# Loading the second MLP weight in five pieces instead of four at the end of a decode block

## The chip, the cores and the metric

One NeuronCore of a Trainium2 chip runs the whole program. The time is the device time of one execution in microseconds (us); "fast" executions are those outside the chip's slower state, and only they are compared. Times from the start of a trace ("at 80.41") count from the first instruction of the profiled execution. A trace spans some 84 us where the device time is some 86. A load is split over 16 DMA engines and counted by 16 increments; it has landed when the last of them has come. Landing times below are taken from these increments in the traces.

## The reference

A decode step of one token for four sequences: adaptive layer norm, cached sliding-window attention, a residual, a second layer norm, and a two-layer MLP with ReLU. Only the last part is touched:

```
def _B_ref(x, w1, w2):            # x [4,1,512], w1 [512,1792], w2 [1792,512]
    h = einsum('bsd,df->bsf', x, w1)
    h = maximum(h, 0)
    return einsum('bsf,fd->bsd', h, w2)
x = x + gb * _B_ref(h, B_w1, B_w2)
```

The inputs are about 32 MB (caches in the window, five weights, all bf16) and each is read once.

## The kernel before

All large loads are issued by SyncE on one queue, in the order in which they are used: k, w_mod, wq, more k, v, wo, w1, and last w2. w2 has 14 blocks of 128 rows. A piece of `e` blocks is laid out so that partition q gets `e` neighbouring rows, one packet of `e` KB. The columns of w1 are then read with step `e`, so that hidden unit and w2 row meet on the same partition.

```
W2_CHUNKS = [(0, 6), (6, 5), (11, 2), (13, 1)]
for (m0, e) in W2_CHUNKS:
    nc.sync.dma_start(out=w2_dst[:, m0 * D:(m0 + e) * D],
                      in_=B_w2[m0 * P:(m0 + e) * P, :].rearrange("(q e) n -> q (e n)", e=e))
...
def w1_cols(t, m):
    m0, e = [ch for ch in W2_CHUNKS if ch[0] <= m][-1]
    return w1_sb[:, t, m0 * P + m - m0:(m0 + e) * P:e]          # step e
...
def ffn1(m0, m1):         # u = w1 columns of blocks m0..m1, then three VectorE operations into uT32
    u_ps = psA.tile(...)
    for m in range(m0, m1):
        for t in range(DT):                                     # 4
            nc.tensor.matmul(out=u_ps[:, m - m0]..., lhsT=w1_cols(t, m), rhs=ab[:, t]..., ...)
    ...
def ffn2(m0, m1):         # z += u block x w2 block, four column groups
    for m in range(m0, m1):
        for nh in range(NH):                                    # 4
            nc.tensor.matmul(out=z_ps[nh * CG:(nh + 1) * CG, :], lhsT=uT32[:, m, :],
                             rhs=w2_sb[:, m, nh * DH2:(nh + 1) * DH2], ...)

for (m0, m1) in [(0, 6), (6, FT)]:
    ffn1(m0, m1)
for (m0, e) in W2_CHUNKS:
    ffn2(m0, m0 + e)
nc.vector.tensor_tensor(out=zg[:], in0=z_ps[:], in1=gb2[:], op=ALU.mult)
nc.vector.tensor_tensor(out=res[:], in0=zg[:], in1=x12_ps[:], op=ALU.add)
nc.sync.dma_start(out=out..., in_=res[::BS, :])
```

Of the kernel before, what the change touches and what calls it, by code (L numbers as in the profile page):

```python
# [17 lines left out]
def kernel(  # L18
# [23 lines left out]
    FT = Dff // P  # L42
# [75 lines left out]
    w2_sb = w12[:, DT * Dff:DT * Dff + FT * D].rearrange("p (m n) -> p m n", m=FT)  # L118
    nc.sync.dma_start(out=w1_sb, in_=B_w1.rearrange("(p t) n -> p t n", t=DT))

    W2_CHUNKS = [(0, 6), (6, 5), (11, 2), (13, 1)]
    assert sum(e for _, e in W2_CHUNKS) == FT
    w2_dst = w12[:, DT * Dff:DT * Dff + FT * D]
    for (m0, e) in W2_CHUNKS:
        nc.sync.dma_start(out=w2_dst[:, m0 * D:(m0 + e) * D],
# [323 lines left out]
    def w1_cols(t, m):  # L449
        m0, e = [ch for ch in W2_CHUNKS if ch[0] <= m][-1]  # L450
        return w1_sb[:, t, m0 * P + m - m0:(m0 + e) * P:e]
# [3 lines left out]
    def ffn1(m0, m1):  # L455
        u_ps = psA.tile([P, m1 - m0, 2, B], f32, tag="t", name=f"u_ps_{m0}")
        for m in range(m0, m1):
            for t in range(DT):
                nc.tensor.matmul(out=u_ps[:, m - m0].rearrange("p s b -> p (s b)"), lhsT=w1_cols(t, m),  # L459
                                 rhs=ab[:, t].rearrange("p s b -> p (s b)"), start=(t == 0), stop=(t == DT - 1))  # L460
        us = work.tile([P, m1 - m0, B], f32, name=f"us_{m0}")
        nc.vector.tensor_tensor(out=us[:], in0=u_ps[:, :, 0, :], in1=rstd2[:].unsqueeze(1).to_broadcast([P, m1 - m0, B]),
                                op=ALU.mult)
        nc.vector.tensor_tensor(out=us[:], in0=us[:], in1=u_ps[:, :, 1, :], op=ALU.add)
        nc.vector.tensor_scalar_max(out=uT32[:, m0:m1, ::BS], in0=us[:], scalar1=0.0)

    def ffn2(m0, m1):
        for m in range(m0, m1):
            for nh in range(NH):
                nc.tensor.matmul(out=z_ps[nh * CG:(nh + 1) * CG, :], lhsT=uT32[:, m, :],  # L470
                                 rhs=w2_sb[:, m, nh * DH2:(nh + 1) * DH2],
                                 start=(m == 0), stop=(m == FT - 1), tile_position=(0, nh * CG))

    for (m0, m1) in [(0, 6), (6, FT)]:
        ffn1(m0, m1)
    for (m0, e) in W2_CHUNKS:
        ffn2(m0, m0 + e)
# [36 lines left out]
```

## Time and profile before

| | before |
|---|---|
| device time, median of 3 (lowest to highest) | 85.94 us (85.81 to 85.98) |
| DMA queue of the loads: packets, MB, share of 16 engines | 4052, 31.99, 91.7% |
| TensorE matmuls busy | 57.5 us, 68% |
| w1 has landed / last piece of w2 has landed | 75.96 / 80.41 us |
| last group of ffn2's matmuls starts | 80.45 us |

The share of TensorE is an average over stages and says little.

### The profile page before, as it was taken

How to read it: one execution, taken by the hardware profiler on the slowest of the kernel's cores; microseconds unless marked ns; L12 is line 12 of the kernel's file. 1: busy time of each engine (PE TensorE's matmuls, PEld its weight loads, DVE VectorE, ACT ScalarE, POOL GpSimd, SP SyncE). 2: the span in 40 equal slices, each digit the busy share in tenths (PEclk: the TensorE clock that was granted, in tenths of full speed). 3: DMA queues.
4: the chain of work that ended last, by engine and by line, in shares of the span. 5: the costliest groups of instructions: out<-in, count | busy, mean ns of one | idle time of the engine just before them, and what ended most of it. 6: DMA issues, size and time to landing. Idle time of an engine off the chain costs nothing.

```text
span 84.1 us, 2367 instructions
## 1 busy us (share of the span) xinstructions
PE 57.5 (68%) x1064; PEld 47.4 (56%) x1064; DVE 26.4 (31%) x73; ACT 23.5 (28%) x37; POOL 5.2 (6%) x20
## 2 busy tenths in 40 slices
PE   0029940499729899999999329996454478598840
PEld 0029940248629739977778029996452058588720
DVE  0144480030330103645665768500003020241420
ACT  2314670003020004977798196300000010001000
POOL 6980000000000000000000000000000000000000
PEclk9999999957955555999999995696555555555555
DMA  0999998999999999999999999999999999999500
GB/s 2 333 401 452 503 421 386 444 421 444 421 394 405 433 433 413 413 413 425 425 413 409 425 425 421 405 433 421 425 409 409 425 432 425 413 398 406 210 0 2
DMA packets 4077, 32.13 MB, mean 382 GB/s; under 512 B 476, under 2 KB 612, under 8 KB 996
## 3 DMA queue, kind: packets, MB, share of 16 engines
q1 hardware_dynamic: 4052, 31.99, 91.7%
q8 instruction: 8, 0.13, 0.6%
q10 hardware_dynamic: 16, 0.01, 0.0%
q14 instruction: 1, 0.01, 0.0%
HBM read 31.99 MB, written 0.00 MB: 381 GB/s over the span
## 4 chain that ended last, share of the span: by engine, by line
DMA 64%; PE 25%; DVE 3%; issue 2%; SPq 1%; ACT 1%; DVEq 0%
DMA w<-in_B_w_dram 24%; DMA v<-in_A_v_cache_dram 24%; DMA wmod_sb<-in_w_mod_dram 16%; PE ktp L202 9%; PE qT_ps L302 4%; PE sc_ps L214 4%; PE mT L253 2%; PE mT L255 2%; PE z_ps L470 2%; PE m_ps L236 2%; SPq L81 1%; PE m_ps L239 1%; PE gb_ps L244 1%; PE st_ps_var L269 1%; ACT lnv L286 0%
## 5 line engine op out<-in xcount | busy, mean ns | idle before, releaser
L202 PEld LDWEIGHTS <-k 128*128 128x128 bf16 x256 | 17.3, 110 | 3.9 <-issue 2.5
L202 PE MATMUL ktp<-ident_k,k 128*128 128x128 bf16 x256 | 18.4, 241 | 1.2 <-DMA k<-in_A_k_cache_dram 1.2
L207 ACT COPY kT<-ktp 128x1024 bf16<-128x1024 bf16 x16 | 15.5, 1016 | 13.2 <-PE ktp L202 12.1
L205 DVE COPY kT<-ktp 128x1024 bf16<-128x1024 bf16 x16 | 11.1, 691 | 11.6 <-PE ktp L202 11.3
L340 PE MATMUL oT_ps<-pT,v 128*128 128x16 bf16 x256 | 7.3, 172 | 2.5 <-issue 1.9
L340 PEld LDWEIGHTS <-v 128*128 128x128 bf16 x256 | 7.1, 100 | 2.7 <-issue 2.0
L214 PE MATMUL sc_ps<-kT,qpad 128*32 128x512 bf16 x64 | 5.6, 445 | 0.4 <-DVE qpad L306 0.4
L357 PE MATMUL pT_ps<-ident_bf,p_rep 128*128 128x128 bf16 x32 | 3.1, 278 | 2.9 <-DVE p_rep L351 2.9
L357 PEld LDWEIGHTS <-p_rep 128*128 128x128 bf16 x32 | 2.7, 127 | 3.4 <-DVE p_rep L351 3.4
L302 PE MATMUL qT_ps<-hT,wq_sb 128*128 128x4 bf16 x128 | 3.6, 166 | 1.4 <-DVE ab L295 1.4
L302 PEld LDWEIGHTS <-wq_sb 128*128 128x128 bf16 x128 | 3.5, 104 | 1.5 <-issue 1.5
L236 PE MATMUL m_ps<-wmod_sb,siluT 128*32 128x512 bf16 x16 | 1.3, 435 | 4.4 <-DMA wmod_sb<-in_w_mod_dram 4.4
L409 ACT COPY y<-y_ps 128x256 f32<-128x256 f32 x1 | 0.4, 372 | 11.4 <-DVE y L408 11.4
L404 PE MATMUL y_ps<-wo_sb,o 128*32 128x512 bf16 x16 | 2.1, 619 | 2.0 <-DMA wo_sb<-in_A_wo_dram 1.1
L177 PE MATMUL tp<-ident_bf,cx_sb 8*128 8x8 bf16 x4 | 0.3, 168 | 4.5 <-DMA cx_sb<-in_A_x_dram 4.5
L236 PEld LDWEIGHTS <-siluT 128*32 128x32 bf16 x16 | 0.4, 95 | 4.7 <-issue 4.5
L382 DVE TENSOR_TENSOR oT_sb<-oT_ps,rb 128x128 bf16<-128x128 f32 x1 | 0.3, 292 | 8.6 <-PE oT_ps L340 8.6
L416 PEld LDWEIGHTS <-wo_sb 128*128 128x128 bf16 x64 | 2.5, 121 | 0.6 <-DMA wo_sb<-in_A_wo_dram 0.6
L416 PE MATMUL y_ps<-o,wo_sb 128*128 128x4 bf16 x64 | 2.4, 173 | 0.5 <-DMA wo_sb<-in_A_wo_dram 0.5
L177 PEld LDWEIGHTS <-cx_sb 8*128 8x128 bf16 x4 | 0.2, 110 | 4.5 <-issue 4.5
L351 DVE TENSOR_TENSOR p_rep<-e_sb,mi 128x512 int32<-128x512 int32 x4 | 2.5, 685 | 0.7 <-ACT e_sb L346 0.7
L459 PE MATMUL u_ps<-ab,w 128*128 128x8 bf16 x56 | 2.4, 181 | 0.4 <-DMA w<-in_B_w_dram 0.4
(107 smaller groups left out, 57.0 us busy)
## 6 DMA issues: line engine op xcount, KB each, us to landing
k<-in_A_k_cache_dram SPq DMA_DIRECT2D x8, 1024.0 KB, 25.8
v<-in_A_v_cache_dram SPq DMA_DIRECT2D x8, 1024.0 KB, 19.9
wq_sb<-in_A_wq_dram SPq DMA_DIRECT2D x2, 2048.0 KB, 18.0
wo_sb<-in_A_wo_dram SPq DMA_DIRECT2D x4, 1024.0 KB, 19.9
wmod_sb<-in_w_mod_dram SPq DMA_DIRECT2D x1, 3072.0 KB, 13.7
w<-in_B_w_dram SPq DMA_DIRECT2D x1, 1792.0 KB, 21.7
w<-in_B_w_dram SPq DMA_DIRECT2D x1, 768.0 KB
w<-in_B_w_dram SPq DMA_DIRECT2D x1, 640.0 KB, 20.1
```

The source lines that it names most:

```text
L202: nc.tensor.transpose(out=tp[:, ii, :], in_=k_tiles[gi][:, iq * IQ + ii, :], identity=ident_k)
L205: nc.vector.tensor_copy(out=dst, in_=tp[:])
L207: nc.scalar.copy(out=dst, in_=tp[:])
L214: nc.tensor.matmul(out=sc_ps[hw * CG:(hw + 1) * CG, half * HALF:(half + 1) * HALF], lhsT=qpad[:, b, par, hw, :], rhs=kT[:, half * (NI // 2 ...
L236: nc.tensor.matmul(out=m4_ps[k * CG:(k + 1) * CG, :], lhsT=siluT32[:, t, :], rhs=wmod_sb[:, t, k * D:(k + 1) * D], start=(t == 0), stop=(t ...
L302: nc.tensor.matmul(out=qT_v[:, hq, :], lhsT=wq_sb[:, t, hq * Dh:(hq + 1) * Dh], rhs=hT[:, t, :], start=(t == 0 and hq == 0), stop=(t == DT ...
L340: nc.tensor.matmul(out=oT_ps[:, hw, par].rearrange("p b r -> p (b r)"), lhsT=v_tiles[h][:, i, :], rhs=pT[:, i, c0:c0 + B * rep], start=(fi ...
L351: nc.vector.tensor_tensor(out=p_w[:, ws, :], in0=e_w[:, ws].unsqueeze(2).to_broadcast([P, WQ // 2, B]), in1=mi4[:].unsqueeze(1).to_broadca ...
L357: nc.tensor.transpose(out=tp[:, ii, :], in_=p_rep[:, i // 2, :, i % 2], identity=ident_bf[:])
L404: nc.tensor.matmul(out=y4_ps[q0:q0 + CG, :], lhsT=o4[:, l, g % 2, g // 2, :], rhs=wo_sb[:, g, l, :], start=(g == 0 and l < 4), stop=(g == ...
L416: nc.tensor.matmul(out=y_ps[:, m, :], lhsT=wo_sb[:, g, l, m::DT], rhs=o4[:, l, g % 2, g // 2, 0:B], start=False, stop=(g == NP - 1 and l = ...
L459: nc.tensor.matmul(out=u_ps[:, m - m0].rearrange("p s b -> p (s b)"), lhsT=w1_cols(t, m), rhs=ab[:, t].rearrange("p s b -> p (s b)"), star ...
```

## The change

The first two pieces, 6 and 5 blocks, become three of 4, 4 and 3, so that ffn2 has fewer blocks to do behind each landing. The last two pieces stay. ffn1's two halves are cut at the border of a piece again, now 8 and 6.

```
-    W2_CHUNKS = [(0, 6), (6, 5), (11, 2), (13, 1)]
+    W2_CHUNKS = [(0, 4), (4, 4), (8, 3), (11, 2), (13, 1)]
...
-    for (m0, m1) in [(0, 6), (6, FT)]:
+    for (m0, m1) in [(0, 8), (8, FT)]:
         ffn1(m0, m1)
```

## The prediction

> **What bounds the kernel now.** I read the page first (shares, slices, the DMA queue), then the chain that ended last in order of time, then the list of DMA issues, then narrow timelines of the last two microseconds. The page says that the stream of loads is the bound:
>
> ```profile
> DMA  0999998999999999999999999999999999999500
> q1 hardware_dynamic: 4052, 31.99, 91.7%
> ```
>
> Each digit is the busy share of the 16 DMA engines in one slice of 2.1 us. They work at 90% or more from the second slice to the 37th, and stop some 4 us before the end. Nearly all the kernel is one read of 32 MB; computation matters only in what is left to do after the last byte. So the case is decided in the last 8 us. The chain ends like this (start us, duration us, what):
>
> ```profile
> 59.28 20.14 DMA w<-in_B_w_dram
> 79.42 0.04 issue
> 79.46 1.31 PE z_ps L470 x30
> 80.77 0.02 issue
> 80.79 0.30 DVE zg L480
> 81.10 0.02 issue
> 81.12 0.29 DVE res L482
> ```
>
> Read at face value this says: the load issued at 59.28 lands at 79.42, and then TensorE works 1.31 us without a wait. The load issued at 59.28 is the second piece of w2 (5 blocks). If that were all, finer pieces would help. But the profile models the ends of pipelined matmuls, so short waits between groups of them vanish in this line. The issues and their landings tell more (KB each, us to landing):
>
> ```profile
> w<-in_B_w_dram SPq DMA_DIRECT2D x1, 640.0 KB, 20.1
> w<-in_B_w_dram SPq DMA_DIRECT2D x1, 256.0 KB, 18.3
> w<-in_B_w_dram SPq DMA_DIRECT2D x1, 128.0 KB, 16.2
> ```
>
> The timeline of the DMA queue has these three issued at 59.28, 61.73 and 64.22, so they land at about 79.42, 80.07 and 80.42. The timeline of TensorE's weight loads in three narrow windows (start, duration, what) agrees:
>
> ```profile
> 79.55 0.44 PEld L470 LDWEIGHTS <-uT 128*32 128x32 bf16 x11
> ...
> 80.11 0.21 PEld L470 LDWEIGHTS <-uT 128*32 128x32 bf16 x8
> ...
> 80.45 0.10 PEld L470 LDWEIGHTS <-uT 128*32 128x32 bf16 x3
> ```
>
> The 20 matmuls of blocks 6 to 10 start within 79.46 to 79.87, the 8 of blocks 11 and 12 at 80.11, the 4 of block 13 at 80.45: each group 0.04 us after its piece has landed. TensorE stands ready for the last piece from about 80.2. What sets the end is therefore the landing of the last piece (80.41), then 4 matmuls, then two VectorE operations of 0.29 us, then the store. Neither the 6 nor the 5 is on that path except by the bytes ahead of the last piece.
>
> The stream runs dry unevenly (columns: us, busy PE, PEld, DVE, ACT, POOL, clock, DMA share, GB/s):
>
> ```profile
> 70.00:78.00 8.00, 6.35 (x146) 6.01 (x146) 2.10 (x13) 0.50 (x2) 0.00 (x0) 0.50 0.99 407
> 78.00:78.50 0.50, 0.50 (x23) 0.48 (x24) 0.11 (x2) 0.00 (x0) 0.00 (x0) 0.50 0.75 270
> 78.50:79.00 0.50, 0.50 (x24) 0.40 (x16) 0.43 (x3) 0.00 (x0) 0.00 (x0) 0.50 0.50 193
> 79.00:79.50 0.50, 0.20 (x12) 0.14 (x8) 0.13 (x1) 0.00 (x0) 0.00 (x0) 0.50 0.45 166
> ```
>
> From 78.0 on the share falls to a half: about half of the engines are done and the others lag. In the trace's records of the last piece's 16 landings, the first is at 78.53 and the last at 80.41.
>
> **What the Trainium skill says.** "DMA: Bandwidth & Descriptors", section "Why a DMA increments its semaphore by 16 and not by 1": a transfer runs on up to 16 engines that finish independently, and only the full count means that all has landed. The trace agrees, with 16 increments 1.88 us apart from first to last; so a piece waits for the laggard, whatever its size. The same page, "Why small descriptors are slow (HBM only)": each packet carries a fixed overhead. The trace agrees in kind: its packet records have medians of 46, 84, 199, 236 and 312 ns for 1, 2, 5, 6 and 8 KB, which is 38 ns a KB and about 8 ns a packet. The same page, "Anatomy of one DMA", names a fixed cost of about 2 us, mostly the receipt of the write. Here the last data packet ends at 79.94 and the landing is at 80.41, only 0.47 us, and pieces behind one another overlap it. "SBUF — State Buffer", section "Door 1: The DMA port swizzle", says that stepping over 16-byte lines costs, and that two hits a line are needed for full rate. This bears on the weight loads of w1, whose step is the piece's number of blocks: 12 bytes at six. The trace agrees that large steps cost, see below.
>
> **The change part by part.**
>
> 1. Pieces. Bytes are the same, the last two pieces are the same. 256 packets (128 of 6 KB, 128 of 5 KB) become 384 (256 of 4 KB, 128 of 3 KB). Per engine that is 8 more data packets x 8 ns = 0.064 us, and one more completion packet of 9 ns: +0.07 us on every engine, at the end of the stream and fully on the path. The last landing goes from 80.41 to 80.48. Worked by piece from w1's landing at 75.96: 4 KB costs 8 x 160 ns and 3 KB 8 x 122 ns, so the pieces should land at about 77.3, 78.55, 79.5, 80.14 and 80.48.
>
> 2. The new issue. The instruction order shows that each load waits for the one eight before it; the fifth piece waits for the second part of wo. In before it was the store that waited for this, until 66.70. So the fifth piece is issued at 66.70 instead of 64.22, still 13 us ahead of its bytes, in a queue that holds some 5 MB. Worth 0.
>
> 3. ffn1. The split 6+8 becomes 8+6. The two triples of VectorE operations swap widths (24 and 32 columns, 183 against 193 ns): 0. The step of the weight loads falls. Loads of w1 in the trace take 144 ns at step 6, 131 at step 5, 104 at steps 2 and 1; the loads of wo on line 416, at step 4, take 118. Their spacing is 46.7, 40.0, 26.7 and 33.3 ns. At step 3 I estimate 26.7 from this line. So ffn1 takes 32 x 33.3 + 24 x 26.7 = 1.71 us where it took 24 x 46.7 + 20 x 40.0 + 12 x 26.7 = 2.24. TensorE gains 0.53 us there, and ends ffn1 at about 77.9 in place of 78.4. But the first half, 8 blocks, ends at about 77.3 by its last matmul, and its three VectorE operations at about 78.0, as now (78.06).
>
> 4. ffn2. Blocks 0 to 3 run at about 78.0, 4 to 7 after 78.6, 8 to 10 after 79.5 (12 matmuls in four column groups, 3 x 0.107 us), 11 and 12 after 80.18, block 13 after 80.52. Before the last landing TensorE is idle again. All the time gained in 3 ends in waits for data: 0 on the path.
>
> 5. The end. The store moves to the next of the eight completion semaphores, the last that the closing sequence waits for. In the trace these waits follow each other by 0.06 us, and in before one more comes after the store's. I expect that one step to be gone: -0.06 us.
>
> Sum: +0.07 + 0 + 0 - 0.06 = +0.01 us, so 85.95.
>
> **The rivals.** (a) The finer pieces do shorten the tail. This is the intent: 5 blocks behind one landing become 3, 8 matmuls fewer at 26.7 ns, 0.21 us; with the 0.53 us of ffn1 at most 0.74 us, or 85.2. For it speaks the chain line of 1.31 us; against it the three groups of weight loads, which start with the landings. (b) Smaller packets and one more completion slow the stream by more than the fit says, because the lagging engines pay a receipt each time: five times 0.47 us exposed in place of four would be +0.5 us, or 86.4. Against it: pieces of 2 KB and 1 KB land 0.65 and 0.34 us after their forerunners, just 8 x 84 and 8 x 46 ns, so nothing is exposed. (c) TensorE becomes the bound: blocks 0 to 7 now wait for one common first half, and run late. They would need to be 0.5 us late before block 13 is delayed; +0 to +0.2 us. (d) The skew of the engines changes: one fetch of instructions (16 KB, started at 78.25) shares an engine with the last pieces. TensorE gets to its fetches at slightly other times, and if one falls on a laggard, the last landing moves by up to 16 x 38 ns = 0.6 us, either way. I see no way to tell beforehand.
>
> **Range and chances.** The three runs of before span 0.17 us. With (d) as the main uncertainty and (b) the more likely of the other sides, 85.65 to 86.35 should hold it 8 times in 10. A change of 2% is 1.7 us, over twice what any rival gives. So within 2%: 0.98, the rest split evenly.
>
> **What would show it.** The page's queue line should count 4052 + 144 = 4196 packets and the same 31.99 MB. The last piece should land at about 80.5, with the final 4 weight loads 0.04 us later; loads of w1 should show 118 ns for the first 32 and about 105 for the rest; ffn1 should end 0.5 us earlier and a wait for DMA stand after it. I am wrong if the last landing comes before 80.3 or after 80.7 for reasons other than packets (then look at the spread of the 16 engines), or if the last group of matmuls starts late after its landing.

## More of the kernel before

One line of the timeline (start us, us, engine, line, operation, operands, count, and the idle time before) shows ffn1:

```profile
76.00 2.32 PEld L459 LDWEIGHTS <-w 128*128 128x128 bf16 x56 [0.52 <-DMA w<-in_B_w_dram]
```

It starts when w1 has landed, and 56 weight loads take 2.32 us.

## The result, and the profile after

| | before | after |
|---|---|---|
| device time, median of 6 | 85.91 us | 85.91 us |
| lowest to highest | 85.81 to 85.98 | 85.83 to 85.93 |
| ratio of the fast runs, 95% interval | | 0.9999 (0.9986 to 1.0012) |

The ratio here and below is the mean time of one kernel's fast runs over that of the other's of the same rounds, so it is not quite the ratio of the medians quoted. The time is the same.

The queue line of the page after the change (packets, MB, share):

```profile
q1 hardware_dynamic: 4196, 31.99, 91.9%
```

There are 144 packets more, 128 of data and 16 of completion, for the same bytes. The issues of w1 and w2 (KB each, us to landing):

```profile
w<-in_B_w_dram SPq DMA_DIRECT2D x1, 1792.0 KB, 21.7
w<-in_B_w_dram SPq DMA_DIRECT2D x2, 512.0 KB, 19.2
w<-in_B_w_dram SPq DMA_DIRECT2D x1, 384.0 KB, 17.8
w<-in_B_w_dram SPq DMA_DIRECT2D x1, 256.0 KB, 16.0
w<-in_B_w_dram SPq DMA_DIRECT2D x1, 128.0 KB, 13.8
```

The last piece is issued at 66.63 and lands 13.8 us later, at 80.44; before, it was issued at 64.22 and took 16.2. It waits less in a queue of the same length. An issue 2.4 us later with the same landing says that the queue was never short of work.

TensorE in the timeline of the changed kernel, and its weight loads of ffn2 in narrow windows (same columns):

```profile
75.96 1.80 PEld L459 LDWEIGHTS <-w 128*128 128x128 bf16 x56 [0.56 <-DMA w<-in_B_w_dram]
...
78.04 0.45 PEld L470 LDWEIGHTS <-uT 128*32 128x32 bf16 x17 [0.28 <-DVE uT L465]
...
78.52 0.42 PEld L470 LDWEIGHTS <-uT 128*32 128x32 bf16 x16
...
79.49 0.32 PEld L470 LDWEIGHTS <-uT 128*32 128x32 bf16 x12 [0.55 <-issue]
...
80.17 0.21 PEld L470 LDWEIGHTS <-uT 128*32 128x32 bf16 x8 [0.36 <-issue]
...
80.48 0.11 PEld L470 LDWEIGHTS <-uT 128*32 128x32 bf16 x3
```

ffn1 takes 1.80 us where it took 2.32. Then come five groups for the five pieces. The first waits 0.28 us for VectorE's uT. The landing records give 78.48, 79.44, 80.12 and 80.44 for the other four pieces, and their groups start 0.04 to 0.05 us behind them. The idle times in front of ffn2's groups, of which those of 0.28, 0.55 and 0.36 us stand in brackets, are where the half microsecond won in ffn1 has gone: added up over all groups they are about 1.3 us, where they were about 0.7 before. TensorE comes earlier and waits longer. (The "issue" in the brackets is the weight load's own sequencer, which names no cause; the landing records name it.)

The chain that ended last now reads:

```profile
64.16 15.96 DMA w<-in_B_w_dram
80.12 0.04 issue
80.16 0.64 PE z_ps L470 x10
80.80 0.02 issue
80.83 0.30 DVE zg L480
```

Before, it said 1.31 us of TensorE after the DMA, now 0.64. Nothing became faster by that difference: zg starts at 80.83 where it started at 80.79. The line only begins at the last gap that the modelled ends of the matmuls leave visible. In both kernels the real last wait is one piece later, in front of block 13.

The whole end of the kernel can be laid out in four terms, each from one trace:

| | w1 landed to last piece landed | to zg | zg to store landed | store landed to end |
|---|---|---|---|---|
| before | 4.45 | 0.39 | 2.40 | 0.89 |
| after | 4.52 | 0.39 | 2.38 | 0.83 |

The first term rose by 0.07 us and the last fell by 0.06. Each column is one trace, but both terms repeat: in the experiments below the six traces with these five pieces give 4.51 to 4.53 for the first, and the two with the old four pieces 4.45.

### The profile page after: what moved, and what is told of

Same layout as the page of the kernel before. It is cut to its first block, busy times and chain, and to the rows that moved or that the text cites. A ratio compares the mean times of both kernels' runs of the same rounds, so it can differ in the third digit from the quotient of the medians.

```text
span 84.0 us, 2368 instructions
## 1 busy us (share of the span) xinstructions
PE 57.2 (68%) x1064; PEld 46.8 (56%) x1064; DVE 26.3 (31%) x73; ACT 23.5 (28%) x37; POOL 5.2 (6%) x20
## 4 chain that ended last, share of the span: by engine, by line
DMA 92%; SPq 2%; PE 1%; DVE 1%; issue 0%
DMA v<-in_A_v_cache_dram 28%; DMA wo_sb<-in_A_wo_dram 24%; DMA wq_sb<-in_A_wq_dram 21%; DMA w<-in_B_w_dram 19%; SPq L81 1%; PE z_ps L470 1%; SPq L90 1%; DVE zg L480 0%; DVE res L482 0%
## 5 line engine op out<-in xcount | busy, mean ns | idle before, releaser
L470 PE MATMUL z_ps<-w,uT 128*32 128x128 bf16 x56 | 2.2, 302 | 0.7 <-DMA w<-in_B_w_dram 0.5
```

## The experiments

Every run was timed in five rounds against the kernel before on the same chip. Each is judged by this ledger too. W is w1's landing to the last piece's, Z is from there to zg, C is the store's landing to the end, from the traces, in us. The last column is the gap between the medians of the same rounds.

| run | W | Z | C | ratio (95%) | medians |
|---|---|---|---|---|---|
| before | 4.45 | 0.39 | 0.89 | | |
| the change | 4.52 | 0.39 | 0.83 | 0.9999 (0.9986 to 1.0012) | 0.00 |
| e1_split_only | 4.45 | 0.39 | 0.89 | 0.9999 (0.9987 to 1.0011) | +0.02 |
| e2_pieces_only | 4.52 | 0.39 | 0.83 | 0.9987 (0.9973 to 1.0001) | -0.01 |
| e3_seven | 4.66 | 0.39 | 1.06 | 1.0042 (1.0029 to 1.0054) | +0.40 |
| e4_last_four | 4.40 | 0.71 | 0.96 | 1.0022 (1.0010 to 1.0034) | +0.27 |
| e5_half_twice | 4.53 | 0.39 | 0.83 | 0.9999 (0.9985 to 1.0013) | -0.04 |
| e6_both_twice | 4.53 | 0.91 | 0.83 | 1.0058 (1.0044 to 1.0072) | +0.46 |
| e7_fewer_bytes | 4.22 | 0.39 | 0.83 | 0.9974 (0.9960 to 0.9987) | -0.27 |
| e8_eight_engines | 4.51 | 0.39 | 0.84 | 1.0008 (0.9995 to 1.0021) | +0.05 |
| e10_nine_fetches | 4.52 | 0.39 | 0.84 | 1.0006 (0.9992 to 1.0020) | +0.08 |

My theory: the end is set by the landing of the last piece, the work behind that landing, and the closing sequence. Rivals: TensorE's work in the tail counts; completions of small pieces cost a receipt each (the time from a piece's last packet to its landing); two real effects cancel.

### One part of the change at a time

e1_split_only is the change with the old list of pieces:

```
-    W2_CHUNKS = [(0, 4), (4, 4), (8, 3), (11, 2), (13, 1)]
+    W2_CHUNKS = [(0, 6), (6, 5), (11, 2), (13, 1)]
```

> Old pieces 6, 5, 2, 1 with the new split of ffn1 (8 and 6 blocks). My theory (the landing of the last piece sets the end): nothing moves on the path, 85.91 us, ratio 1.000 within 0.002; last landing near 80.41, last matmul group 0.04 us after it. Rival (the later first half of ffn1 holds ffn2 back): the first group of ffn2 starts near 78.7 instead of 78.34, and if that mattered the time would be up to 0.3 us more.

The ratio is 0.9999. Last landing and last group are 0.26 us later in this trace than in the kernel before, but so is w1's landing (76.22): the stream as a whole ran late, and W is 4.45 in both. The split does nothing on the path. The rival is tested less hard than was expected: counted from w1's landing, ffn2's first group starts only 0.11 us later than before (78.71 after 76.22, against 78.34 after 75.96), where some 0.36 had been forecast.

e2_pieces_only is the change with the old split:

```
-    for (m0, m1) in [(0, 8), (8, FT)]:
+    for (m0, m1) in [(0, 6), (6, FT)]:
```

> New pieces 4, 4, 3, 2, 1 with the old split of ffn1 (6 and 8 blocks). My theory: same sum as the whole change, +0.07 us of packets on the last landing and -0.06 us in the closing waits, so 85.92 us, ratio 1.000 within 0.002. ffn1 still ends 0.5 us earlier than in the kernel before, since the step of the weight loads goes with the pieces and not with the split. Rival (the whole change hides two real effects that cancel, pieces faster and split slower): this run 0.2 to 0.7 us faster and the one with the split alone slower by as much.

0.9987, with an interval that holds 1; W and C are those of the whole change. ffn1's last matmul starts at 77.79, as expected some 0.5 us earlier than before (78.24). So the two parts do not hide a gain and a loss of 0.2 us or more each. A tenth of a us cannot be told apart by these rounds.

### More pieces

e3_seven cuts the first 11 blocks into 2, 2, 2, 2 and 3:

```
-    W2_CHUNKS = [(0, 4), (4, 4), (8, 3), (11, 2), (13, 1)]
+    W2_CHUNKS = [(0, 2), (2, 2), (4, 2), (6, 2), (8, 3), (11, 2), (13, 1)]
```

> Seven pieces 2, 2, 2, 2, 3, 2, 1. My theory: against the kernel before 24 more data packets an engine at 8 ns and 3 more completions at 9 ns, so the last landing is 0.22 us later after w1's; the store now sits on the second of the closing waits, three steps of 0.06 us more than before. Sum +0.40 us, 86.3 us, ratio 1.0047. Rival (each completion is exposed as a receipt of 0.47 us): +1.4 us, ratio 1.016. Rival (finer is faster): below 85.9.

The queue line counts 432 packets more than before, three times 144:

```profile
q1 hardware_dynamic: 4484, 31.99, 91.6%
```

W is +0.21 us against +0.22 expected, C +0.17 against +0.18, the ratio 1.0042 against 1.0047. An exposed receipt of 0.47 us for each completion is ruled out, and so is a gain from finer pieces. The cost of a piece is its packets (8 x 8 ns an engine) and one completion packet of 9 ns. The closing term is no property of pieces: it depends on which of the eight completion semaphores the store comes to use, and the closing sequence asks for them in a fixed order, about 0.06 us a step. With seven pieces the store has the second, so the rest come after it.

### Work behind the last landing

e4_last_four makes the last piece four blocks long:

```
-    W2_CHUNKS = [(0, 4), (4, 4), (8, 3), (11, 2), (13, 1)]
+    W2_CHUNKS = [(0, 6), (6, 4), (10, 4)]
```

> Three pieces 6, 4, 4, so that four blocks instead of one stand behind the last landing. My theory: the last landing 0.07 us earlier against w1's than in the kernel before, then 16 matmuls instead of 4, three groups of 0.107 us more, +0.32, and one closing step of 0.06 more: +0.31 us, 86.2 us, ratio 1.0036. Rival (only the bytes of the stream count): -0.07 us, ratio 0.999.

The timeline of its last matmuls:

```profile
80.37 0.62 PE L470 MATMUL z_ps<-w,uT 128*32 128x128 bf16 x16 [0.62 <-DMA w<-in_B_w_dram]
80.37 0.34 PEld L470 LDWEIGHTS <-uT 128*32 128x32 bf16 x15 [0.81 <-issue]
81.03 0.29 DVE L480 TENSOR_TENSOR zg<-z_ps,gb 128x128 f32<-128x128 f32 x1 [2.01 <-PE z_ps L470]
```

All 16 start behind the landing at 80.33, and zg comes 0.71 us after it instead of 0.39: +0.32, as worked out. W is -0.05 and C +0.06, so the sum of these three is +0.33, or +0.30 with the time from zg to the store's landing, which is 2.37 here and 2.40 before. The timed runs show less of it: 0.0022 of 86 us is 0.19, with the interval from 0.09 to 0.29 just short of the expected 0.31, and the medians differ by 0.27. The direction and the term Z are shown; the missing tenth of the timed ratio is open. It is of the size by which w1's landing moves from trace to trace (75.87 to 76.22). This is the piece whose size does count, and the change left it alone.

### Slack of TensorE

e5_half_twice repeats the second half of ffn1 (the first pass's sums are overwritten), e6_both_twice repeats both:

```
-    def ffn1(m0, m1):
+    def ffn1(m0, m1, times=1):
...
-        for m in range(m0, m1):
+        for m in list(range(m0, m1)) * times:
...
-        ffn1(m0, m1)
+        ffn1(m0, m1, 1 if m0 == 0 else 2)     # e6_both_twice: 2
```

> The changed kernel with the second half of ffn1 computed twice: 24 more pairs of weight load and matmul at 26.7 ns, 0.64 us more TensorE work; the result stays right. My theory: ffn1 ends near 78.3 instead of 77.7, all of it goes into the waits for the pieces, the last group of matmuls still starts 0.04 us after the last landing: 85.93 us, ratio 1.000 within 0.002. Rival (TensorE is on the path in the tail, so work given or taken there counts): +0.6 us, ratio 1.0075.

```profile
75.91 2.42 PEld L459 LDWEIGHTS <-w 128*128 128x128 bf16 x80 [0.55 <-DMA w<-in_B_w_dram]
...
80.78 0.29 DVE L480 TENSOR_TENSOR zg<-z_ps,gb 128x128 f32<-128x128 f32 x1 [1.67 <-PE z_ps L470]
```

Ffn1's last matmul starts at 78.26 instead of 77.68, and nothing happens to the end: 0.9999, Z 0.39. As much TensorE work as the change saves can be put back for nothing.

> Both halves of ffn1 computed twice: 56 more pairs, 1.71 us more TensorE work. My theory: now the slack is used up. ffn1 ends near 79.4, the second half's VectorE operations near 80.2 to 80.3, so blocks 8 to 13 run after that: the last group starts near 80.9 instead of 80.48, +0.4 us, ratio 1.005 (1.003 to 1.007), and the last group no longer follows a landing. Rival (never on the path): 1.000. Rival (always on the path): +1.7 us, ratio 1.020.

Ratio 1.0058, Z 0.91 instead of 0.39. The chain of this kernel (start us, us, what):

```profile
75.95 0.05 issue
76.00 3.58 PE u_ps L459 x112
79.58 1.79 PE z_ps L470 x55
81.39 0.30 DVE zg L480
```

This is what the chain looks like when TensorE really bounds the tail: one unbroken run of TensorE work from w1's landing to zg, the last landing at 80.48 not in it. ffn1's last matmul starts 1.73 us later than in the changed kernel (79.41 against 77.68) and zg 0.52 us later against the landing. So of this additional work about 1.2 us are free, and it explains why 0.5 us won there was worth nothing. The prediction counted slack otherwise, by how late blocks 0 to 7 may run: counted so, ffn2's first matmul starts 1.44 us later against w1's landing (79.51 after 75.95, against 78.04 after 75.92), so about 0.9 us are free, where the prediction said 0.5.

### Bytes in the stream

e7_fewer_bytes loads three blocks in the first piece instead of four. Its output is wrong, which doesn't matter for the time.

```
-    for (m0, e) in W2_CHUNKS:
+    for (m0, e) in [(0, 3)] + W2_CHUNKS[1:]:
         nc.sync.dma_start(...)
...
-                                 rhs=w2_sb[:, m, nh * DH2:(nh + 1) * DH2],
+                                 rhs=w2_sb[:, 2 if m == 3 else m, nh * DH2:(nh + 1) * DH2],
```

> The changed kernel, its first w2 piece loaded with 3 blocks instead of 4, and block 3 read from block 2 (a wrong result on purpose). Same packets, same TensorE work, 128 KB less in the stream, 8 KB an engine. My theory: every landing after it comes 8 x 38 ns = 0.30 us earlier and the end with it: 85.6 us, ratio 0.9965. Rival (something other than the last landing sets the end): 1.000.

```profile
q1 hardware_dynamic: 4196, 31.86, 91.7%
...
76.15 1.78 PEld L459 LDWEIGHTS <-w 128*128 128x128 bf16 x56 [0.57 <-DMA w<-in_B_w_dram]
...
80.71 0.29 DVE L480 TENSOR_TENSOR zg<-z_ps,gb 128x128 f32<-128x128 f32 x1 [2.00 <-PE z_ps L470]
```

The packets are as many and the bytes 0.13 MB fewer. W falls from 4.52 to 4.22, by 0.3 us as expected, and zg starts 4.56 us after ffn1's first weight load instead of 4.87. The ratio is 0.9974, whose interval holds the expected 0.9965. The end moves with the last landing. Since TensorE's work is the same, this and e5_half_twice together show which of the two sets the time.

### Two questions about the skew of the DMA engines

The skew is the time between the first and the last increment of a piece. In every trace some engines finish the stream 1.5 us or more ahead of the latest, and the last piece waits for that one. e8_eight_engines tried to use that; the intent was that eight engines alone carry the last two pieces, as the grouping of their rows might bring about:

```
+        w2_in = B_w2[m0 * P:(m0 + e) * P, :].rearrange("(q e) n -> q (e n)", e=e)
+        if m0 >= 11:
+            w2_in = w2_in.rearrange("(a r) x -> a r x", a=8)
```

> The changed kernel with the source of the last two pieces (blocks 11 to 13) given as 8 groups of 16 rows[...]; the result stays right. An attempt to use the skew: in the trace 8 engines are done 1.5 to 1.9 us before the rest. If those 8 are the lowest-numbered, the last landing comes up to 0.9 us earlier, 85.0 to 85.5 us, ratio 0.990 to 0.995. If they are the laggards, +0.9 us, ratio 1.010. If mixed, between 1.003 and 1.010. If the rule does not take these shapes, 16 engines and 1.000. The count of landings [...]tells which: 8 in place of 16 for the last two pieces.

The last two pieces still land in 16 steps each, and the ratio is 1.0008: the attempt missed. The 8 groups of 16 rows lie one behind the other, and the issued instruction shows no trace of the grouping (its form is the same as before). So the intended transfer was not tried. Whether the early engines are the low-numbered ones stays open, and so does the gain.

e10_nine_fetches asks what makes the laggards:

```
+    for _ in range(128):
+        nc.tensor.matmul(out=m4_ps[0:CG, 0:8], lhsT=siluT32[:, 0, :], rhs=ident_bf[:, 0:8],
+                         start=True, stop=True, tile_position=(0, 0))
```

> The changed kernel with 128 small extra pairs of weight load and matmul while TensorE waits for w_mod (their result is overwritten). It asks where the skew of the DMA engines comes from: in the traces one more engine falls behind by about 1.3 us or more after most instruction fetches of 16 KB, and 8 of 16 are late at the end. If fetches make the laggards, 256 more instructions[...] are one fetch more: 9 packets on the instruction queue and 9 of the 16 landings of the last piece late by over a us. The last landing is the latest of any engine and stays where it is if the ninth hits a fresh engine: 85.93 us, ratio 1.000 within 0.003; if it hits a late one, about +1.3 us, ratio 1.015. If fetches are not the cause: 8 late landings, ratio 1.000.

The instruction queue of this kernel:

```profile
q8 instruction: 9, 0.15, 0.7%
```

It was 8 packets in the changed kernel, the first at 21.82. Here the first is at 16.39. In the landing records of the changed kernel the first load with one straggler is the one that ends at 26.87 us (1.5 us behind the other 15); here it is the one before, ending at 21.94 (1.15 us behind). The late engines stay late in the loads that follow, and their number grows. Up to w1's landing the changed kernel, like nine others of the eleven traces, has 7 fetches and 8 increments that come 0.9 us or more behind the first; this one has 8 fetches and 9. At the last piece, 9 of 16 increments come from 79.69 on, where it was 8 from 79.93 on. So one fetch more makes one laggard more, from the moment of the fetch on.

Not all of it is explained: in the changed kernel a seventh late increment comes at 68.61, in a load that ends at 69.11, though only six fetches have started by then, and the last fetch (78.36 there, 79.97 here) adds no late one. That 8 fetches and 8 late increments are the same number is therefore chance. The last landing against w1's did not move (4.52), and the time is the same; one of the six executions, 87.45 us, was slow and is left out.

No version beat both kernels: the smallest ratio of a correct one is that of e2_pieces_only, and its interval holds 1.

## Why the prediction was right

- What bounds: the last landing, not the 1.31 us of TensorE that the chain showed. Borne out by e5_half_twice (more TensorE work, no effect) and e7_fewer_bytes (fewer bytes, full effect). One reading of the page was loose: the seventh slice of the DMA line is an 8, not 90% or more; nothing rests on it.
- Step 1, +0.07 us of packets: W went from 4.45 to 4.52. The pieces were expected at 77.3, 78.55, 79.5, 80.14 and 80.48, and landed at 77.20, 78.48, 79.44, 80.12 and 80.44, 0.04 us of it from an earlier w1. (The prediction's packet costs alone, added up from 75.96, would give 80.54 for the last; its 80.48 is the old landing plus 0.07, and that is what came.) e3_seven confirmed the rate with three times the pieces.
- Step 2, the later issue, worth 0: issued at 66.63, landed in line.
- Step 3, ffn1 1.71 us: its first and last matmul start 1.72 us apart. The loads at step 4 take 118 ns as expected. Those at step 3 were guessed at 26.7 ns apart; they came 28 apart in this trace and 26.7 in that of e3_seven, without consequence.
- Step 4, everything gained goes into waits: the idle times in front of ffn2's groups, of 0.55 and 0.36 us for data and, besides, 0.28 us for VectorE.
- Step 5, one closing step less: C went from 0.89 to 0.83.
- The rivals: (a) fell with e1_split_only, e2_pieces_only and e5_half_twice; (b) with e3_seven; (c) is real but begins only when blocks 0 to 7 are about 0.9 us late, where the prediction said 0.5 (e6_both_twice); (d) did not come about: the last piece's increments spread over 1.88 us before and 1.83 after, and over 1.75 to 2.11 us in all eleven traces. Its size was put too low. The prediction took 16 KB at 38 ns a KB, 0.6 us, but the trace that it read has 1.11 us for the fetch at 78.25, and a first straggler was 1.15 to 1.5 us behind. Since the prediction saw no way to tell whether a fetch would meet a laggard, that none did is luck.

The predicted 85.95 us stands against 85.91 us, inside the spread of a single kernel's runs. The +0.01 of the sum is below what the rounds can show; its two terms are seen in the traces alone. One comparison is not like with like: the section that the prediction cites for a fixed cost of about 2 us is about DMAs issued by GpSimd, and the loads with 0.47 us here are issued by SyncE.

## What to carry to other kernels

When a stream of loads bounds a kernel, ask of each piece whether it is the last one: only the bytes ahead of the last landing and the work behind it are on the path, and pieces in the middle may be cut otherwise at the price of their packets (here four, five and seven pieces in all), as long as the engine that uses them keeps its slack. A chain that shows a long run of TensorE after a DMA may hide several short waits, because the ends of matmuls are modelled; look for groups of weight loads that start right behind landings before believing it. To learn how much slack an engine has, give it work twice until the time moves.

## What the Trainium skill lacked or had wrong

- "TensorE: Matmul & The Clock Gate", section "LDWEIGHTS (loading the stationary operand)", gives a time by the number of columns alone; for 128 columns its formula makes an estimate of 107 ns. The records agree at steps 1 and 2 of the column (104 ns), but at the same 128 columns and the same granted clock of 0.50 a load took 118 ns at step 4, 131 at 5 and 144 at 6. The loads followed each other every 26.7 ns at steps 1 and 2, 26.7 to 28 at 3 (e3_seven, the changed kernel), 33.3 at 4, 40.0 at 5 and 46.7 at 6.
- "SBUF — State Buffer", section "Door 1: The DMA port swizzle (why `[64,N]` ≈ `[32,N]`)", says that two hits in a 16-byte line are enough for full rate. For weight loads that did not hold: step 4 in bf16 has two in a line and was at 33.3 ns in place of 26.7.
- "DMA: Bandwidth & Descriptors", section "Anatomy of one DMA — SWDGE (gpsimd) path", has a fixed cost of about 2 us for the path of GpSimd. The section has no such figure for loads into SBUF issued by SyncE; here 0.47 us passed from the end of the last packet to the landing, and pieces in a full queue overlap even that (e3_seven, +0.07 us a piece).
- "Runtime: NRT & Kernel Launch", section "Instruction fetch mechanics", has the fetches as blocks of 16 KiB on a DMA queue of their own and their cost as mostly hidden. Neither it nor another page that was found tells that they make stragglers of the engines that carry the loads: in the two kernels 8 fetches of 16 KB, each taking about 1.02 to 1.11 us, and an engine that falls 1.15 to 1.5 us behind in the next landing (the changed kernel and e10_nine_fetches).
- No page that was found tells that the closing sequence waits for the completion semaphores one after the other, 0.06 us a step, so that it matters which of them the last store uses (0.83 us after the store's landing in the changed kernel, 1.06 in e3_seven).
